# Linear attention and a two-layer block on one core: q ahead of k and a denominator without v in the opening, a bf16 spread, one more batch transposed by DMA, the last tile in two halves

## The chip, the cores and the metric

One core of one Trainium2 chip. The time is device microseconds of one execution, the median of several. The granted clock is the share of its full clock that the profile shows TensorE to have had. The four runs of each kernel in the result lie within 0.15% of each other; in the later jobs those of the kernel before spread over 0.4 to 0.9%, the longest of them (304.88 and 304.77 us) with a mean clock of 0.991. "Faster" and "slower" mean by 2% or more.

## The reference, cut to what matters

```python
phi = lambda x: np.where(x > 0, x, np.exp(x) - 1.0) + 1.0        # q, k, v: (8, 8, 576, 64)
q_p, k_p = phi(q), phi(k)
kv  = einsum('bhsd,bhse->bhde', k_p, v);   z = k_p.sum(axis=2)
attn = einsum('bhsd,bhde->bhse', q_p, kv) / (einsum('bhsd,bhd->bhs', q_p, z)[..., None] + 1e-6)
x = attn.transpose(0, 2, 1, 3).reshape(4608, 512)
h = x @ w_in;  out = (h - np.tanh(h)) @ w_out                     # (512, 2048), (2048, 512)
```

## The kernel before

The dense part runs in nine stages of 512 tokens: a first layer (64 matmuls of 512 columns) and a second (64 more). The attention of batch n+1 is woven into stage n as small pieces, at the end of the tiles of the first layer (`s1`) and of the groups of four matmuls of the second (`s2`). Batch 0 has nothing to hide behind: it is the opening. In the traces each engine's rows come in the order of the program, so where a piece stands in the text decides what it waits behind.

The pieces of a batch have these names: phi of q and of k (ScalarE's exp, then a max and a min on VectorE), q transposed (`qT`), `kv` and z, the denominator and 1/den (`rden`), the numerators (`num`, products of q and kv), the spread (each 1/den copied to all rows of its head), and the scaling of the numerators by it into `xT`, the input of the dense part. `w_in` and `w_out` are the weights of the two layers. TensorE writes its products to PSUM, which the kernel lays out as eight banks (`ps_all`).

```python
    load_k(0); load_q(0); load_v(0)          # all of these are issued from POOL, in this order
    make_identity(nc, ident)
    for g in range(4): load_wi(g)
    nc.gpsimd.memset(sel, 0.0)               # fp32 selector [128, 4, 2, 64], four affine selects
    ...
    load_k(1); load_wo(0); load_q(1); load_wo(1); load_v(1); load_wo(2); load_wo(3)

    def a_spread(b):                         # batches 2 to 7: 1/den through DRAM, broadcast by DMA
        ds = dram.tile([H, 4, J * 16], F32, name="ds")
        for t in range(4): nc.sync.dma_start(out=ds[:, t, :], in_=rden_t[b][32*t:32*t+H, :])
        ...                                  # two broadcasts ds -> rdb
    def a_spread_pe(b, bank0, pairs):        # batches 0 and 1: by TensorE into four PSUM banks
        ...  nc.tensor.matmul(bp[...], sel[r, p], rden_t[b][r], start=True, stop=True)
    ...
        if c == 0:                           # stage 0
            ...
            s2[9].append(num1); s2[11].append(lambda: spread1(0)); s2[13].append(lambda: spread1(1))
            s2[14].append(lambda: a_qphi(2, 0)); s2[15].append(lambda: a_qphi(2, 1))
        if c == 1:
            for n in range(4):               # batch 2 transposed by TensorE in stage 1
                s1[4 + n].append(lambda n=n: a_qT_pe(2, n // 2, attn, (n % 2,)))
        ...
            for p in range(NP + 1): s2[9 + p].append(lambda p=p: a_num(n1, p))   # needs rdb
```

## Time and profile before

| | us |
|---|---|
| median (303.03 to 303.42, 4 runs) | 303.19 |
| first dense matmul | 19.89 |
| stage 0, from there to the first matmul of stage 1 | 33.39 |
| first layer of stage 1 | 19.05 |
| second layer of stage 1 (72.33 to 87.12) | 14.79 |
| stages 2 to 8, to the start of the last output copy (296.45) | 209.33 |
| from that copy to the end of the span | 4.85 |

The lengths add up to the span of 301.3 us. The table is read from starts of instructions: the profile models the ends of matmuls, so a pause of TensorE costs about 0.16 us more, start to start, than the idle time that a row shows (a matmul of 512 columns is drawn 0.38 us long, and the next one starts 0.216 us after it).

### The profile page before, as it was taken

The numbers are of one execution on the slowest core, as the hardware profiler recorded it, in microseconds if no ns is written. First come the engines' busy times: TensorE is split into PE (matmuls) and PEld (weight loads), VectorE is DVE, ScalarE is ACT, GpSimd is POOL, SyncE is SP. The second block draws the span as 40 slices with busy tenths as digits, with TensorE's granted clock in tenths as the row PEclk, the third lists the DMA queues.
The fourth block names the chain that finished last, engine by engine and source line by source line (L and its number), as shares of the span: only waits on it lengthen the run. The fifth ranks groups of instructions, "written<-read, shape, count | busy, mean of one in ns | idle before, by whom it ended". The sixth has DMA issues, their size and how long they took to land.

```text
span 301.3 us, 4706 instructions
## 1 busy us (share of the span) xinstructions
PE 291.9 (97%) x1790; PEld 138.3 (46%) x1790; DVE 180.2 (60%) x304; ACT 149.6 (50%) x230; POOL 52.1 (17%) x91
## 2 busy tenths in 40 slices
PE   8989999989999999999999999999999999999993
PEld 3454454444445444544454445444544444444441
DVE  7658944887557854785478557865681467008500
ACT  3638914954734653565256625662562166136420
POOL 8873263051006000600050003000000000000000
PEclk9999999999999999999999999999999999999999
DMA  6999999677969786967697778477108310130033
GB/s 90 189 207 206 205 207 205 181 120 135 212 111 177 122 200 138 155 116 190 140 151 135 179 148 128 87 173 148 38 4 193 71 35 0 37 86 18 2 70 70
DMA packets 36406, 38.23 MB, mean 127 GB/s; under 512 B 14432, under 2 KB 31008, under 8 KB 35616
## 3 DMA queue, kind: packets, MB, share of 16 engines
q0 software_dynamic: 17600, 18.35, 37.8%
q1 hardware_dynamic: 18784, 19.58, 29.0%
q8 instruction: 14, 0.23, 0.3%
q14 instruction: 8, 0.07, 0.1%
HBM read 43.78 MB, written 9.55 MB: 177 GB/s over the span
## 4 chain that ended last, share of the span: by engine, by line
PE 79%; DMA 9%; DVE 5%; ACT 2%; issue 1%; POOL 1%; SPq 0%; DVEq 0%; POOLq 0%; ACTq 0%
PE ps_all L270 38%; PE ps_all L285 33%; DMA qraw<-in_q_dram 4%; PE ps_all L166 4%; DMA out_dram<-osb 2%; DVE gT L276 2%; PE ps_all L221 2%; DMA v<-in_v_dram 2%; ACT e L127 1%; ACT osb L290 1%; DVE kp L129 1%; PE ps_all L191 1%; POOL kraw L85 1%; DVE r L128 1%; DVE qp L129 1%
## 5 line engine op out<-in xcount | busy, mean ns | idle before, releaser
L285 PE MATMUL ps_all<-w_out_sb,gT 128*128 128x512 bf16 x576 | 131.6, 379 | 0.0
L270 PE MATMUL ps_all<-xT,w_in_sb 128*128 128x512 bf16 x576 | 128.5, 379 | 0.2 <-DVE xT L263 0.2
L276 DVE TENSOR_TENSOR gT<-ps_all,th 128x512 bf16<-128x512 f32 x144 | 96.8, 687 | 53.0 <-ACT th L275 52.6
L275 ACT ACTIVATE th<-ps_all 128x512 f32<-128x512 f32 x144 | 85.3, 600 | 51.7 <-PE ps_all L270 47.2
L285 PEld LDWEIGHTS <-gT 128*128 128x128 bf16 x576 | 55.5, 98 | 65.7 <-issue 0.2
L270 PEld LDWEIGHTS <-w_in_sb 128*128 128x128 bf16 x576 | 55.2, 98 | 65.9 <-issue 1.1
L290 ACT COPY osb<-ps_all 128x512 f32<-128x512 f32 x36 | 21.1, 586 | 79.6 <-PE ps_all L285 59.5
L232 DVE TENSOR_TENSOR xT<-ps_all,rdb 128x512 bf16<-128x512 f32 x24 | 16.4, 689 | 11.8 <-PE ps_all L221 11.8
L104 POOL DMA_DIRECT2D v<-in_v_dram x32 | 19.2, 615 | 18.7 <-PE ps_all L166 5.7
L127 ACT ACTIVATE e<-kraw 128x1152 bf16<-128x1152 bf16 x16 | 18.5, 1165 | 5.1 <-DMA kraw<-in_k_dram 5.1
L129 DVE TENSOR_TENSOR kp<-e,r 128x1152 bf16<-128x1152 bf16 x16 | 12.1, 759 | 14.1 <-ACT e L127 13.0
L127 ACT ACTIVATE e<-qraw 128x1152 bf16<-128x1152 bf16 x16 | 18.4, 1166 | 0.9 <-DMA qraw<-in_q_dram 0.9
L129 DVE TENSOR_TENSOR qp<-e,r 128x1152 bf16<-128x1152 bf16 x16 | 12.1, 758 | 8.1 <-ACT e L127 7.3
L281 POOL COPY g<-gT 1x1 bf16<-1x1 bf16 x4 | 0.7, 176 | 92.9 <-DVE gT L276 92.9
L166 PE MATMUL ps_all<-v,kp 64*128 64x192 bf16 x288 | 13.7, 243 | 0.0
L166 PEld LDWEIGHTS <-kp 64*128 64x128 bf16 x288 | 11.5, 94 | 3.5 <-issue 2.9
L338 PE MATMUL ps_all<-zero 128*128 128x512 bf16 x36 | 10.4, 461 | 1.2 <-DVE zero L297 1.2
L221 PE MATMUL ps_all<-qT,kz 128*128 128x512 bf16 x32 | 11.3, 380 | 0.0
L89 POOL DMA_DIRECT2D kraw<-in_k_dram x14 | 8.7, 628 | 11.8 <-ACT qT L157 10.4
L89 POOL DMA_DIRECT2D qraw<-in_q_dram x14 | 8.7, 642 | 5.9 <-DVE r L128 5.9
L263 DVE TENSOR_TENSOR xT<-ns,ps_all 128x576 bf16<-128x576 f32 x8 | 5.6, 750 | 5.0 <-PE ps_all L258 5.0
L175 DVE TENSOR_TENSOR kz<-ps_all,mask 128x320 bf16<-128x320 f32 x14 | 6.2, 485 | 3.7 <-PE ps_all L166 3.7
(45 smaller groups left out, 92.8 us busy)
## 6 DMA issues: line engine op xcount, KB each, us to landing
out_dram<-osb SPq DMA_DIRECT2D x72, 128.0 KB
rdb<-ds SPq DMA_DIRECT2D x12, 576.0 KB
v<-in_v_dram POOLq DMA_DIRECT2D x32, 144.0 KB, 6.7
kraw<-in_k_dram POOLq DMA_DIRECT2D x14, 288.0 KB, 5.0
qraw<-in_q_dram POOLq DMA_DIRECT2D x14, 288.0 KB, 6.8
w_in_sb<-in_moe_w_in_dram POOLq DMA_DIRECT2D x4, 512.0 KB, 10.1
w_out_sb<-in_moe_w_out_dram POOLq DMA_DIRECT2D x4, 512.0 KB, 12.1
kraw<-in_k_dram POOLq DMA_DIRECT2D x4, 144.0 KB, 3.8
```

The source lines that it names most:

```text
L89: nc.gpsimd.dma_start(out=t[64 * hg:64 * hg + 64].rearrange("p i h j d -> p (i h) (j d)"), in_=src[b, 4 * hg:4 * hg + 4].rearrange("h (p j ...
L104: nc.gpsimd.dma_start(out=v_b[b % 2][64 * hg:64 * hg + 64, i, 0:2].rearrange("p h j d -> p h (j d)"), in_=v[b, h0:h0 + 2].rearrange("h (p ...
L127: nc.scalar.activation(e, x, AF.Exp)
L129: nc.vector.tensor_tensor(store[b][:, i].rearrange("p j h d -> p h j d"), e, r, ALU.min)
L166: nc.tensor.matmul(ps[hg], kp[r, i, j].rearrange("p h d -> p (h d)"), vt[r, i, :, j, :], start=(j == 0), stop=(j == J - 1))
L221: nc.tensor.matmul(ps, kz[:, p // 2, p % 2, 0:128], qT[:, p % 2, 0:8, p // 2, :], start=True, stop=True)
L232: nc.vector.tensor_mul(xT[:, p, S * b:S * b + 512].rearrange("p (j t c) -> p j t c", j=8, t=4), ps.rearrange("p j (t c) -> p j t c", t=4), ...
L270: nc.tensor.matmul(h, w_in_sb[:, p, fi * 128:(fi + 1) * 128], xT[:, p, c * 512:(c + 1) * 512], start=(p == 0), stop=(p == NP - 1))
L275: nc.scalar.activation(th, h, AF.Tanh)
L276: nc.vector.tensor_sub(gT[:, fi, :], h, th)
L285: nc.tensor.matmul(o, gT[:, fi, i * 128:(i + 1) * 128], w_out_sb[:, fi, :], start=(fi == 0), stop=(fi == NF - 1))
L290: nc.scalar.copy(osb, o)
```

## The change

It means to shorten the opening (q first, then k; z from k alone, so that the denominator no longer waits for v; selectors built small), to take TensorE work out (batch 2's transposes; batch 1's spread in bf16 in place of fp32), and to shorten the end. Batch 1's pieces in stage 0 stand a step or two later than before, batch 2's kv and denominator in stage 1 one or two steps earlier. The core of the diff:

```diff
-    load_k(0); load_q(0); load_v(0); make_identity(nc, ident)
+    load_q(0); make_identity(nc, ident); load_k(0); load_v(0)
+    nc.gpsimd.memset(s8, 0.0)                    # three small selectors [128, 3, 4, 2]
+    for n in range(3):
+        for t in range(4): nc.gpsimd.affine_select(out=s8[r, n], ...)
     for g in range(4): load_wi(g)
-    nc.gpsimd.memset(sel, 0.0)
-    for t in range(4): nc.gpsimd.affine_select(out=sel[r], ...)
...                                               # the opening: z, kv, numerators of batch 0 in pieces
+    def a_split(b):                              # 1/den as three bf16 parts, rows 0-7, 8-15, 16-23
...
-  sel[r, p], rden_t[b][r]
+  (sel3 if b else sel)[r, p], rden_t[b][r]       # bf16 for batch 1
...
+            s2[9].append(lambda: (a_den(1, side), a_split(1)))
+            s2[12].append(lambda: spread1(0));  s2[13].append(lambda: a_qphi(2, 0))
+            s2[14].append(lambda: spread1(1));  s2[15].append(lambda: (a_qphi(2, 1), a_qT_dma(2)))
...
-            for n in range(4): s1[4 + n].append(lambda n=n: a_qT_pe(2, n // 2, attn, (n % 2,)))
-            s1[9 if c == 1 else 5].append(lambda: a_kv(n1, attn))
-            s1[11 if c == 1 else 8].append(lambda: (a_den(n1, attn), a_spread(n1)))
+            s1[7 if c == 1 else 5].append(lambda: a_kv(n1, attn))
+            s1[10 if c == 1 else 8].append(lambda: (a_den(n1, attn), a_spread(n1)))
-            s1[3].append(lambda: (a_kphi(2, 1), load_k(3), load_q(3)))   # stage 1
-            if c + 3 < B: s1[10].append(lambda: load_v(c + 3))
+            s1[0].append(lambda: (gate(gT, 0), load_k(n2), load_q(n2), load_v(n2)))
...
+            if c == NC - 1 and i == 3: ...       # last tile in two halves of 256 columns
```

More of the change, by code (lines that the diff above doesn't have):

```diff
@@ L67 @@
     sel = const.tile([128, NP, 2, 64], F32, name="sel")
+    sel3 = const.tile([128, NP, 2, 64], BF16, name="sel3")
+    s8 = const.tile([128, 3, NP, 2], F32, name="s8")
+    part = const.tile([128, 2], F32, name="part")
     zero = const.tile([128, 512], BF16, name="zero")
@@ L118, with phi_pieces @@
     kp_t, qp_t, qT_t, kz_t, rdb_t, rden_t = {}, {}, {}, {}, {}, {}
-    def phi(b, src, store, name, i):
+    def phi_pieces(b, src, store, name, i):
         if i == 0:
@@ L126, in phi @@
         r = epool.tile([128, 2, J, D], BF16, name="r")
-        nc.scalar.activation(e, x, AF.Exp)
-        nc.vector.tensor_scalar(r, x, 0.0, 1.0, ALU.max, ALU.add)
-        nc.vector.tensor_tensor(store[b][:, i].rearrange("p j h d -> p h j d"), e, r, ALU.min)
+        y = store[b][:, i].rearrange("p j h d -> p h j d")
+        return (lambda: nc.scalar.activation(e, x, AF.Exp),
+                lambda: nc.vector.tensor_scalar(r, x, 0.0, 1.0, ALU.max, ALU.add),
+                lambda: nc.vector.tensor_tensor(y, e, r, ALU.min))
+    def phi(b, src, store, name, i):
+        for f in phi_pieces(b, src, store, name, i):
+            f()
     def a_kphi(b, i):
@@ L144, in a_qT_dma, with a_qT_pe @@
             in_=qp_t[b].rearrange("p i j h d -> p (i j h d)"))
-    def a_qT_pe(b, i, banks, parts=(0, 1)):
-        if i == 0 and 0 in parts:
+    def a_qT_pe(b, i, banks, on=None):
+        if i == 0:
             new_qT(b)
-        for n in parts:
+        for n in range(2):
             j0, j1 = ((0, 5), (5, 9))[n]
@@ L155, in a_qT_pe @@
             dst = qT_t[b][:, i, j0:j1].rearrange("p j g t -> p j (g t)")
-            if n == 0:
+            if (on or "AV")[n] == "A":
                 nc.scalar.copy(dst, src)
@@ L175, in a_kv, with b0_z, b0_zc, b0_kv @@
             nc.vector.tensor_mul(kz_t[b][:, hg], ps[hg][:, :, 0:160], mask[:, hg])
-    def a_kv_half(b, i, banks):
-        if i == 0:
-            kz_t[b] = work.tile([128, 2, 2, 160], BF16, name="kz")
-        ps = [banks()[:, 0:192] for hg in range(2)]
-        kv_mm(b, i, ps)
-        for hg in range(2):
-            nc.vector.tensor_mul(kz_t[b][:, hg, i, :], ps[hg][:, 0:160], mask[:, hg, i, :])
+    def b0_z(i):
+        for j in range(J):
+            for hg in range(2):
+                r = slice(64 * hg, 64 * hg + 64)
+                nc.tensor.matmul(ps_all[:, 2 * i + hg, 0:32], kp_t[0][r, i, j].rearrange("p h d -> p (h d)"),
+                                 one[r, 0:32], start=(j == 0), stop=(j == J - 1))
+    def b0_zc(i):
+        nc.vector.tensor_mul(kz_t[0][:, :, i, 128:160], ps_all[:, 2 * i:2 * i + 2, 0:32], mask[:, :, i, 128:160])
+    def b0_kv(i):
+        for j in range(J):
+            for hg in range(2):
+                r = slice(64 * hg, 64 * hg + 64)
+                nc.tensor.matmul(ps_all[:, 4 + 2 * i + hg, 0:128], kp_t[0][r, i, j].rearrange("p h d -> p (h d)"),
+                                 v_b[0][r, i, 0:2, j, :], start=(j == 0), stop=(j == J - 1))
+    def b0_kz(i):
+        nc.vector.tensor_mul(kz_t[0][:, :, i, 0:128], ps_all[:, 4 + 2 * i:6 + 2 * i, 0:128], mask[:, :, i, 0:128])
+    def b0_num(i, ns, rem):
+        kz, qT = kz_t[0], qT_t[0]
+        for hg in range(2):
+            nc.tensor.matmul(ps_all[:, rem, 64 * hg:64 * hg + 64], kz[:, hg, i, 0:128], qT[:, i, 8, hg, :],
+                             start=True, stop=True)
+        for hg in range(2):
+            nc.tensor.matmul(ps_all[:, 4 + hg, :].rearrange("p (j t) -> p j t", j=8), kz[:, hg, i, 0:128],
+                             qT[:, i, 0:8, hg, :], start=True, stop=True)
+        nc.scalar.copy(ns[:, i::2, 8, :], ps_all[:, rem, 0:128].rearrange("p (a t) -> p a t", a=2))
+        nc.scalar.copy(ns[:, i::2, 0:8, :].rearrange("p a j t -> p a (j t)"), ps_all[:, 4:6, :])
     def a_den(b, banks):
@@ L203, in a_den @@
         rden_t[b] = rden
+    def a_split(b):
+        f = rden_t[b]
+        t1 = rpool.tile([128, J * 16], BF16, name="t1")
+        u = rpool.tile([128, J * 16], F32, name="u")
+        t2 = rpool.tile([128, J * 16], BF16, name="t2")
+        w = rpool.tile([128, J * 16], BF16, name="w")
+        nc.vector.tensor_copy(t1, f)
+        nc.vector.scalar_tensor_tensor(u, t1, part[:, 0:1], f, ALU.mult, ALU.add)
+        nc.vector.tensor_copy(t2, u)
+        nc.vector.scalar_tensor_tensor(w, t2, part[:, 1:2], u, ALU.mult, ALU.add)
+        rden_t[b] = w
     def a_spread(b):
@@ L257, in a_spread_pe @@
                 r = slice(32 * t, 32 * t + 32)
-                nc.tensor.matmul(bp[:, t, 144 * n:144 * n + 144], sel[r, p].rearrange("p h e -> p (h e)"),
+                nc.tensor.matmul(bp[:, t, 144 * n:144 * n + 144], (sel3 if b else sel)[r, p].rearrange("p h e -> p (h e)"),
                                  rden_t[b][r], start=True, stop=True)
@@ L266, in a_scale, with l1mm @@
             bp[:, :, o:o + 144].rearrange("p t (j c) -> p t j c", c=16))
-    def l1mm(c, fi, h, p):
+    def l1mm(c, fi, h, p, n):
         nc.tensor.matmul(h, w_in_sb[:, p, fi * 128:(fi + 1) * 128], xT[:, p, c * 512:(c + 1) * 512],
-                         start=(p == 0), stop=(p == NP - 1))
+                         start=(n == 0), stop=(n == NP - 1))
     def l1act(fi, h, gT):
@@ L286, in l2mm, with evac @@
                              start=(fi == 0), stop=(fi == NF - 1))
-    def evac(c, i, o):
+    def evac(c, i, o, f0=0, f1=None):
+        f1 = DM if f1 is None else f1
         osb = opool.tile([128, DM], F32, name="osb")
-        nc.scalar.copy(osb, o)
+        nc.scalar.copy(osb[:, f0:f1], o[:, f0:f1])
         for half in range(2):
             b, j = divmod(2 * (4 * c + i) + half, J)
-            nc.sync.dma_start(out=out[b * S:(b + 1) * S, :].rearrange("(p j) m -> p j m", j=J)[:, j, :],
-                              in_=osb[64 * half:64 * half + 64])
+            nc.sync.dma_start(out=out[b * S:(b + 1) * S, f0:f1].rearrange("(p j) m -> p j m", j=J)[:, j, :],
+                              in_=osb[64 * half:64 * half + 64, f0:f1])
     nc.vector.memset(zero, 0.0)
@@ L299 @@
     nc.scalar.activation(act0, zero[:, 0:1], AF.Exp)
+    load_q(0)
+    make_identity(nc, ident)
     load_k(0)
-    load_q(0)
     load_v(0)
-    make_identity(nc, ident)
+    nc.gpsimd.memset(s8, 0.0)
+    for n in range(3):
+        for t in range(4):
+            r = slice(32 * t, 32 * t + 32)
+            nc.gpsimd.affine_select(
+                out=s8[r, n], in_=s8[r, n], compare_op=ALU.not_equal, fill=1.0, base=-8 * n,
+                channel_multiplier=1, pattern=[[-1, NP], [-4, 2]])
     for g in range(4):
         load_wi(g)
-    nc.gpsimd.memset(sel, 0.0)
-    for t in range(4):
-        r = slice(32 * t, 32 * t + 32)
-        nc.gpsimd.affine_select(
-            out=sel[r], in_=sel[r], compare_op=ALU.not_equal, fill=1.0, base=0,
-            channel_multiplier=1, pattern=[[-1, NP], [-4, 2], [0, 64]])
     load_k(1)
@@ L325 @@
             nc.vector.memset(mask[64 * hh:64 * hh + 64, p // 2, p % 2, m:m + 1], 1.0)
-    for i in range(2):
-        nc.vector.memset(v_b[i][:, :, 2], 1.0)
+    for n in (1, 2):
+        nc.vector.tensor_copy(mask[:, :, :, 128 + 8 * n:136 + 8 * n], mask[:, :, :, 128:136])
     nc.vector.memset(one, 1.0)
@@ L331 @@
     for n in range(3):
-        part = float(np.float32(rest).astype(ml_dtypes.bfloat16))
-        nc.vector.memset(eps[32 * n:32 * n + 1], part)
-        rest -= part
-    for n in range(36):
-        nc.tensor.matmul(ps_all[:, n % 4, :], zero[:, 0:128], zero, start=True, stop=True)
-    for i in range(2):
-        a_kphi(0, i)
-    for i in range(2):
-        a_qphi(0, i)
-    side, kvb = Banks([4, 5, 6, 7]), Banks([0, 1, 2, 3])
-    a_qT_pe(0, 0, side)
-    a_kv_half(0, 0, kvb)
-    a_qT_pe(0, 1, side)
@@ L347 @@
-    ns0 = new_ns(0)
-    for p in (0, 2):
-        a_num_copy(0, ns0, p, side)
-    a_kv_half(0, 1, kvb)
-    a_den(0, Banks([0]))
-    a_num_copy(0, ns0, NP, Banks([1]))
-    for p in (1, 3):
-        a_num_copy(0, ns0, p, side)
-    bp_a = a_spread_pe(0, 0, (0,))
-    bp_b = a_spread_pe(0, 4, (1, 2, 3))
-    for p in range(NP):
-        a_scale(0, p, ns0, bp_b if p else bp_a, 144 * (p - 1) if p else 0)
+        e0 = float(np.float32(rest).astype(ml_dtypes.bfloat16))
+        nc.vector.memset(eps[32 * n:32 * n + 1], e0)
@@ new lines, with spin @@
+        rest -= e0
+    def spin(n):
+        for _ in range(n):
+            nc.tensor.matmul(ps_all[:, 2, :], zero[:, 0:128], zero, start=True, stop=True)
+    side = Banks([4, 5, 6, 7])
+    kz_t[0] = work.tile([128, 2, 2, 160], BF16, name="kz")
+    (eq0, rq0, mq0), (eq1, rq1, mq1) = (phi_pieces(0, q_t, qp_t, "qp", i) for i in range(2))
+    for f in (eq0, rq0, mq0, eq1, rq1):
+        f()
+    spin(18)
+    a_qT_pe(0, 0, side, "AA")
+    (ek0, rk0, mk0), (ek1, rk1, mk1) = (phi_pieces(0, k_t, kp_t, "kp", i) for i in range(2))
@@ new lines @@
+    for f in (mq1, rk0, ek0):
+        f()
+    spin(6)
+    a_qT_pe(0, 1, side, "VV")
+    for f in (ek1, rk1, mk0):
+        f()
+    nc.scalar.copy(sel, s8[:, 0].unsqueeze(3).to_broadcast([128, NP, 2, 64]))
+    spin(8)
+    b0_z(0)
+    mk1()
+    b0_zc(0)
+    b0_kv(0)
+    b0_kz(0)
+    b0_z(1)
+    b0_zc(1)
+    a_den(0, Banks([0]))
+    ns0 = new_ns(0)
+    b0_num(0, ns0, 1)
+    b0_kv(1)
+    bp_a = a_spread_pe(0, 0, (0, 2))
+    b0_kz(1)
+    b0_num(1, ns0, 6)
+    bp_b = a_spread_pe(0, 4, (1, 3))
@@ new lines @@
+    for n, p in enumerate((0, 2, 1, 3)):
+        a_scale(0, p, ns0, (bp_a, bp_b)[n // 2], 144 * (n % 2))
+    nc.vector.memset(v_b[1][:, :, 2], 1.0)
+    nc.vector.memset(v_b[0][:, :, 2], 1.0)
+    s24 = rpool.tile([128, NP, 2], F32, name="s24")
+    nc.vector.tensor_add(s24, s8[:, 1], s8[:, 2])
+    nc.vector.tensor_reduce(part[:, 0:1], s24.rearrange("p a h -> p (a h)"), mybir.AxisListType.X, ALU.add, negate=True)
+    nc.vector.tensor_reduce(part[:, 1:2], s8[:, 2].rearrange("p a h -> p (a h)"), mybir.AxisListType.X, ALU.add, negate=True)
@@ L359 @@
+    nc.vector.tensor_add(s24, s24, s8[:, 0])
+    nc.vector.tensor_copy(sel3, s24.unsqueeze(3).to_broadcast([128, NP, 2, 64]))
     load_q(2)
@@ L375, in spread1 @@
                     a_scale(1, p, sub["ns"], sub["bp"], 144 * (p % 2))
-            s1[11].append(lambda: a_kphi(1, 0))
-            s1[13].append(lambda: a_kphi(1, 1))
-            s1[15].append(lambda: a_qphi(1, 0))
-            s2[1].append(lambda: a_qphi(1, 1))
-            s2[4].append(lambda: a_qT_pe(1, 0, side))
-            s2[5].append(lambda: a_qT_pe(1, 1, side))
-            s2[6].append(lambda: a_kv(1, side))
-            s2[8].append(lambda: a_den(1, side))
             def num1():
@@ L388, in num1 @@
                     a_num_copy(1, sub["ns"], p, side)
-                load_v(3)
-            s2[9].append(num1)
-            s2[11].append(lambda: spread1(0))
-            s2[13].append(lambda: spread1(1))
-            s2[14].append(lambda: a_qphi(2, 0))
-            s2[15].append(lambda: a_qphi(2, 1))
+            s1[13].append(lambda: a_kphi(1, 0))
+            s1[15].append(lambda: a_kphi(1, 1))
+            s2[1].append(lambda: a_qphi(1, 0))
+            s2[3].append(lambda: a_qphi(1, 1))
+            s2[5].append(lambda: a_qT_pe(1, 0, side))
+            s2[6].append(lambda: a_qT_pe(1, 1, side))
+            s2[7].append(lambda: a_kv(1, side))
+            s2[9].append(lambda: (a_den(1, side), a_split(1)))
+            s2[10].append(num1)
+            s2[12].append(lambda: spread1(0))
+            s2[13].append(lambda: a_qphi(2, 0))
+            s2[14].append(lambda: spread1(1))
+            s2[15].append(lambda: (a_qphi(2, 1), a_qT_dma(2)))
         elif n1 < B:
-            s1[9 if c == 1 else 5].append(lambda: a_kv(n1, attn))
-            s1[11 if c == 1 else 8].append(lambda: (a_den(n1, attn), a_spread(n1)))
+            s1[7 if c == 1 else 5].append(lambda: a_kv(n1, attn))
+            s1[10 if c == 1 else 8].append(lambda: (a_den(n1, attn), a_spread(n1)))
             for p in range(NP + 1):
                 s2[9 + p].append(lambda p=p: a_num(n1, p))
-            if c + 3 < B:
-                s1[10].append(lambda: load_v(c + 3))
         if c == 1:
             s1[1].append(lambda: a_kphi(2, 0))
-            s1[3].append(lambda: (a_kphi(2, 1), load_k(3), load_q(3)))
-            for n in range(4):
-                s1[4 + n].append(lambda n=n: a_qT_pe(2, n // 2, attn, (n % 2,)))
+            s1[3].append(lambda: a_kphi(2, 1))
         if c >= 1 and n2 < B:
-            if c > 1:
-                s1[0].append(lambda: (gate(gT, 0), load_k(n2), load_q(n2)))
-            d = 4 if c == 1 else 2
+            s1[0].append(lambda: (gate(gT, 0), load_k(n2), load_q(n2), load_v(n2)))
+            d = 2
             s2[d].append(lambda: a_kphi(n2, 0))
@@ L420 @@
             first = Banks([4, 5, 6, 7, 0, 1, 2, 3])
-            for p in range(NP):
+            for n, p in enumerate((0, 2, 1, 3)):
                 for fi in range(4):
-                    l1mm(c, fi, hs[fi], p)
+                    l1mm(c, fi, hs[fi], p, n)
             for fi in range(4):
@@ L428 @@
             for p in range(NP):
-                l1mm(c, fi, h, p)
+                l1mm(c, fi, h, p, p)
             l1act(fi, h, gT)
@@ L438 @@
                 os_[i] = ps_all[:, i, :] if c == 0 else dense()
+            if c == NC - 1 and i == 3:
+                if g == 0:
+                    o2 = dense()
+                    for u, o in enumerate((os_[i], o2)):
+                        f = slice(256 * u, 256 * u + 256)
+                        for fi in range(NF):
+                            nc.tensor.matmul(o[:, f], gT[:, fi, 384:512], w_out_sb[:, fi, f],
+                                             start=(fi == 0), stop=(fi == NF - 1))
+                        evac(c, i, o, 256 * u, 256 * u + 256)
+                continue
             l2mm(gT, os_[i], i, 4 * g, 4 * g + 4)
```

## The prediction

> **What bounds the kernel now.** I read the page first, then the chain of waits, then a table of stretches cut at the stage borders, then timelines of the two places where TensorE was not fed. The first line of the page and the table say that TensorE is the bound:
>
> ```profile
> PE 291.9 (97%) x1790; PEld 138.3 (46%) x1790; DVE 180.2 (60%) x304; ACT 149.6 (50%) x230; POOL 52.1 (17%) x91
> ...
> 19.89:53.28 33.39, 33.39 (x238) 16.48 (x238) 22.54 (x38) 18.58 (x31) 11.85 (x20) 1.00 1.22 206
> 53.28:72.33 19.05, 17.31 (x136) 8.77 (x134) 15.80 (x29) 13.90 (x22) 4.84 (x8) 1.00 0.82 159
> ...
> 87.28:103.27 15.99, 15.99 (x118) 7.79 (x116) 11.72 (x19) 9.54 (x16) 5.03 (x9) 1.00 0.95 162
> ```
>
> The three stretches are stage 0 (from its first first-layer matmul to the first of stage 1), the first layer of stage 1, and the first layer of stage 2. The second number is the length, the third TensorE's busy time. In stage 0 and stage 2 they are equal: every removed matmul counts there. The first layer of stage 1 takes 3.06 us more than that of stage 2, and 1.74 us of it is idle TensorE. The waits in that stretch name what fed it late, PE transposes of batch 2 whose PSUM banks were still being read:
>
> ```profile
> PE ps_all L153 <- ACT qT L157: 1.0, 1, 1.0
> PE ps_all L153 <- DVE qT L159: 0.7, 1, 0.7
> ```
>
> Before 19.89 us nothing of the dense work runs. The chain of waits through that opening reads:
>
> ```profile
> 14.04 0.68 PE ps_all L153 x9
> 14.71 0.51 PE ps_all L221 x2
> 15.22 0.89 PE ps_all L166 x18
> 16.12 0.32 DVE kz L183
> ...
> 16.49 0.47 PE ps_all L191 x8
> ...
> 17.08 1.07 DVE rden L202
> ...
> 18.28 0.71 PE ps_all L258 x6
> ...
> 19.08 0.77 DVE xT L263
> ```
>
> So: last phi, transposes, kv, mask, denominator, reciprocal, spread, scaling, and then the dense layers, 5.9 us after the last phi (13.98). From 72.33 us on the chain is TensorE alone, to the last output copy at 296.45.
>
> **What the Trainium skill says.** "TensorE: Matmul & The Clock Gate", section "Back-to-back issue gap", gives N/2.4 + 2.5 ns, 215.8 ns for 512 columns; the trace agrees (the chain has 64 in 13.81 us, 215.8 each). For 256 columns that gives 109 ns, so cutting the last tile in two costs about 32*109 - 16*216 = 0.04 us. The same page, section "Architectural detail: the array is 16× 32×32, not 1× 128×128", says that ScalarE and VectorE are strict FIFO; in the timeline each engine's rows follow the program's order, and below it matters twice. "FP8 and Floating Point Precision", section "TensorE Precision Notes", says true fp32 takes four passes; the trace shows the cost, below. "ScalarE: Activation LUTs", section "What ACT_TABLE_LOAD costs", gives 186 + 0.833N ns for an ACTIVATE; the copies of 512 columns measure 586 to 600 against 612, near enough to use it for new sizes: 128 columns 0.29 us, 1024 columns 1.04.
>
> **The change part by part.**
>
> 1. Batch 2's transposes go from TensorE to DMA. That removes 18 matmuls (1.65 us in this stretch) and the waits above (1.74). The first layer of stage 1 then holds what stage 2's holds, so 19.05 falls to about 15.99: **-3.06 us**. The DMA transpose takes 2.75 us on SyncE's queue, and in later batches about as long again to land. It starts after the last phi of q (near 6.5 us after my mark X below) and is needed by the denominator near X+15.8: some 3 to 4 us to spare.
>
> 2. Batch 1's spread in bf16. Now:
>
> ```profile
> 48.31 0.77 PE L258 MATMUL ps_all<-rden,sel 32*128 32x144 f32 x16
> 49.01 0.60 PE L285 MATMUL ps_all<-w_out_sb,gT 128*128 128x512 bf16 x2
> ```
>
> From 48.31 to the next matmul are 0.70 us for 16 recorded fp32 matmuls. In bf16 there are 8; the denominator's 16 bf16 matmuls, also 144 columns and four at a time, take 0.36 us, so 8 take about 0.18. Two calls: 2*(0.70-0.18) = **-1.0 us** on TensorE. Four small VectorE instructions come on between reciprocal and spread, about 1 us in all (144 columns each, the den add is 0.30); the reciprocal used to end 2.1 us before the spread, so that hides.
>
> 3. The order around the end of stage 0. Call X the end of the matmuls of step 12. The steps then are: spread and scaling of two pairs at 12, phi of q2's first half at 13, spread and scaling of the other two at 14, phi of the second half at 15. VectorE is in order: the second two scalings stand behind the min of step 13's phi, which waits for its exp, which stands on ScalarE behind the output copy of step 13. Durations from the trace: copy 0.59, exp 1.17, min 0.76, scaling 0.71. Step 13's matmuls end at X+1.06 (spread 0.2, then 4*0.216), copy to X+1.85, exp to X+3.0, min to X+3.85, scalings to X+4.6 and X+5.3. The first layer of stage 1 would start at X+3.0 and wants pair 2 at X+3.4. So it waits about 1.2 and 0.5 us: **+1.7 us**. Before, both scalings ended (53.10) just as stage 1 began (53.28). This is the wait that takes the place of the one removed.
>
> 4. The opening. Loads arrive in order of issue, the limit being DMA; the first uses of the eight k and q pieces now are at 5.15, 8.5, 10.24 and 11.73 for each half. With q first, q fills the early places and k the late. ScalarE then: exp of q1 to 9.67, two qT copies (0.69+0.59) to 10.95, exp of k0 to 12.1, of k1 to 13.3; VectorE's min of k1 ends near 14.1, about where the last phi ends now. From there, with z as its own narrow matmuls: z1 at 14.4, denominator 15.2 to 15.8, reciprocal to 16.9, first spread to 17.7, first scaling to 18.5. That alone would start the dense layer at about 18.6, 1.3 us earlier. But TensorE's program has more ahead of it: kv1 (to 16.95), num1 after the mask of kv1 (17.6) to 18.2, ScalarE's 128- and 1024-column copies of num1 to about 19.4, and only then the second spread, which writes banks 4 and 5 that this copy reads, with 0.7 us. The dense layer starts at about 20.2: **+0.3 us**, between -1.3 and +0.8.
>
> 5. Removed from the opening: two memsets of 1.02 us and the wide fp32 selector on POOL. They and the bf16 selector, some 3 us of VectorE, now run after the scalings; VectorE is then behind at the start of stage 0 but has 8 banks of room, and at 0.69 against 0.86 us per tile it catches up before the second layer. The twelve small selects on POOL (an estimate: 0.15 us each, between the 0.29 and 0.71 of wider ones) put the weight loads 2 us later in issue; the first was issued at 9.84 and took 7.2 to land, queued behind the inputs, so it should land as before, near 17.1. No effect.
>
> 6. The last tile is cut in two 256-column halves, so the last copy has 256 columns, not 512: 0.37 instead of 0.59 us, and half the bytes in the last two stores. **-0.3 us**.
>
> 7. k, q and v loaded together one stage ahead: VectorE and ScalarE find them early enough as now; no effect.
>
> Sum: -3.06 - 1.0 + 1.7 + 0.3 - 0.3 = -2.4, from 303.2 to 300.8. Point 4 is the only one where I doubt my bookkeeping on both sides, and an order called tuned has probably been measured; I lean 0.5 us to the good there: **300.3 us**.
>
> **The rivals.** (a) The opening really is shortened: the k chain without v's wait gains 1.3 us and the second spread does not hold it up. For it: the change's intent, and 18.6 for the first scaling. Against it: the bank that the second spread shares with num1. Total about 299.2. (b) No wait at the start of stage 1, because the phi at step 13 finds ScalarE free sooner: total about 298.7. Against it: both engines are in order. (c) VectorE becomes the bound of stage 1's first layer: it has 15.8 us of work in the 19.05 now, and the same work would have to fit in 16; with only 6 dense banks a lag of more than 4 us stalls TensorE. Total 301.5. (d) The DMA transpose lands late behind the output stores and holds up the denominator: 1 to 3 us, total 302 to 303.
>
> **Range and chances.** All terms are below 3.1 us. All gains together without any loss, with rival (a), give 303.2 - 3.06 - 1.0 - 1.3 - 0.3 = 297.5; all losses at once give about 303. I take 298.2 to 302.3. More than 2% is 6.1 us, which needs more than everything counted: 5%. Slower by 2% has no mechanism: 2%.
>
> **What would show each step.** The first dense matmul at 20.2 (18.6 if rival a), and what it waited for; two idle gaps of TensorE, 1.2 and 0.5 us, within the first four matmuls of stage 1, released by VectorE's scaling; its first layer at 16 us plus these gaps, no PE transposes in it; 8 bf16 spread matmuls in about 0.2 us; the last copy at 0.37 us. Wrong would make it: a stage-0 transposition of batch 1 that waits for phi of q, now later behind VectorE's new work, or the two DMA rivals.

## The result

302.78 us (302.62 to 303.01, 4 runs) against 303.19 for the kernel before: a ratio of 0.9987, 95% interval 0.9969 to 1.0004, so no change. A ratio here is the mean time of one kernel's fast runs over that of the other's of the same rounds, so not quite the ratio of the medians. The prediction's range was 298.2 to 302.3.

First the engines' line of the page and the table of stretches of the changed kernel, cut at the same events as before: stage 0 and the two layers of stage 1. A row has start and end, the length, then the busy time and count of TensorE, its weight loads, VectorE, ScalarE and POOL, then the granted clock, the DMA share and GB/s.

```profile
PE 288.7 (96%) x1804; PEld 137.2 (46%) x1804; DVE 181.9 (60%) x313; ACT 149.6 (50%) x229; POOL 52.9 (18%) x100
...
20.25:54.08 33.83, 32.63 (x223) 15.63 (x223) 24.00 (x46) 19.53 (x31) 10.47 (x16) 1.00 1.22 207
54.08:71.36 17.28, 16.30 (x117) 7.76 (x116) 16.09 (x28) 12.36 (x20) 5.01 (x9) 1.00 0.93 173
71.36:87.72 16.36, 14.95 (x73) 6.75 (x72) 8.87 (x15) 6.58 (x8) 0.00 (x0) 1.00 0.83 179
```

Before, the first two stretches read as the prediction shows them, and the third:

```profile
72.33:87.12 14.79, 14.79 (x73) 6.78 (x72) 8.76 (x16) 6.58 (x8) 0.00 (x0) 1.00 0.62 137
```

TensorE's busy time fell by 3.2 us, 1.0 of it four warm-up matmuls fewer in the opening. So TensorE has less work. But in each of these three stretches its busy time is now below the length. In stage 0 and the second layer of stage 1 there were no gaps before; in the first layer of stage 1 the old ones (1.74) have given place to others. The list of TensorE's waits names them, as total, count and longest (the warm-up's is left out, and two of 0.5 and 0.4 in the opening):

```profile
PE ps_all L318 <- DMA w_in_sb<-in_moe_w_in_dram: 1.4, 1, 1.4
PE ps_all L269 <- DVE xT L280: 1.4, 1, 1.4
PE ps_all L333 <- DMA w_out_sb<-in_moe_w_out_dram: 1.2, 1, 1.2
...
PE ps_all L306 <- ACT ns L218: 1.1, 1, 1.1
PE ps_all L318 <- DVE xT L311: 1.0, 2, 0.7
```

In order of time: the second spread of the opening waits for a copy (1.1), the first dense matmul for w_in (1.4), the second layer of stage 0 for w_out (1.2), the first matmuls of stage 1 for the scalings (0.7 and 0.3), a numerator of stage 1 for xT (1.4). The account against the kernel before:

| | before | changed | difference | predicted |
|---|---|---|---|---|
| first dense matmul | 19.89 | 20.25 | +0.36 | +0.3 |
| stage 0 | 33.39 | 33.83 | +0.44 | -1.0 |
| first layer of stage 1 | 19.05 | 17.28 | -1.77 | -1.4 |
| second layer of stage 1 | 14.79 | 16.36 | +1.57 | 0 |
| to the last output copy | 209.33 | 209.37 | +0.04 | 0 |
| from it to the end | 4.85 | 4.11 | -0.74 | -0.3 |

The sum is -0.1 us of span, where -2.4 was reckoned. What was not foreseen stands mainly in two places: stage 0, where the bf16 spread's gain was there and a wait for w_out ate it, and the second layer of stage 1, where nothing had been expected.

**The weight loads.** POOL's rows, before:

```profile
9.84 3.00 POOL L110 DMA_DIRECT2D w_in_sb<-in_moe_w_in_dram  x4
12.80 0.78 POOL L306 MEMSET sel<- 128x512 f32 x1
13.65 3.04 POOL L309 TENSOR_SCALAR_AFFINE_SELECT sel<-sel 32x512 f32<-32x512 f32 x4
```

and of the changed kernel:

```profile
9.25 4.22 POOL L358 TENSOR_SCALAR_AFFINE_SELECT s<-s 32x8 f32<-32x8 f32 x12
13.43 3.03 POOL L113 DMA_DIRECT2D w_in_sb<-in_moe_w_in_dram  x4
```

The twelve selects have 8 columns each in place of 512, but they are twelve, take 4.22 us, and now stand ahead of the weight loads, which are issued at 13.43 in place of 9.84. The DMA queues ran dry just then: in quarters of a microsecond the GB/s go from 198 at 12.50 to 14 at 13.50, and are back at 176 only at 16.00, some 2.5 us after the first of these issues began. The stretch from 13 to 16 us, first before, then changed:

```profile
13.00:16.00 3.00, 2.98 (x47) 2.06 (x45) 2.07 (x6) 1.95 (x4) 2.75 (x4) 1.00 1.23 205
```

```profile
13.00:16.00 3.00, 2.83 (x84) 1.82 (x81) 2.31 (x6) 1.28 (x2) 2.95 (x6) 1.00 0.37 35
```

The loads up to stage 0's second layer follow one another at 200 GB/s or so, so what is lost at 13 us is still missing at 38: w_in's first part lands at 20.20 (17.06 before), the second part of w_out at 38.84 (36.23 before).

**The start of stage 1.** VectorE and TensorE in the timeline of the changed kernel (start, length, instruction; in brackets the idle time ahead of it and what ended it):

```profile
53.89 0.76 DVE L133 TENSOR_TENSOR qp<-e,r 128x1152 bf16<-128x1152 bf16 x1 [0.78 <-ACT e L131]
...
54.57 1.41 DVE L311 TENSOR_TENSOR xT<-ns,ps_all 128x576 bf16<-128x576 f32 x2
...
55.37 0.38 PE L318 MATMUL ps_all<-xT,w_in_sb 128*128 128x512 bf16 x1 [0.69 <-DVE xT L311]
...
56.03 6.42 PE L318 MATMUL ps_all<-xT,w_in_sb 128*128 128x512 bf16 x29 [0.29 <-DVE xT L311]
```

The scalings follow the min of the phi, which waited for ScalarE's exp, as step 3 had it. From the first matmul (54.08) to the third (55.37) are 1.29 us instead of 0.43, to the fourth 0.66 instead of 0.22: 1.30 us lost.

**The broadcast of 1/den of batch 2.** In the second layer of stage 1:

```profile
82.98 1.89 DVE L280 TENSOR_TENSOR xT<-ps_all,rdb 128x512 bf16<-128x512 f32 x3 [2.07 <-DMA rdb<-ds]
...
83.72 0.38 PE L269 MATMUL ps_all<-qT,kz 128*128 128x512 bf16 x1 [1.41 <-DVE xT L280]
```

VectorE waits for the DMA `rdb`; the third numerator needs a PSUM bank that VectorE has not read. Before, the first such scaling started at 81.79 with no idle time ahead of it. TensorE now comes to its numerators 0.96 us sooner (80.00 against 80.96), but the broadcast comes later. The four stores of 1/den that it reads go out 1.8 us sooner than before, yet it can be issued only 0.7 us later than before. First before, then changed:

```profile
71.25 1.34 SPq L209 DMA_DIRECT2D ds<-rden  x4
73.68 1.13 SPq L212 DMA_DIRECT2D rdb<-ds  x2
81.79 1.35 DVE L232 TENSOR_TENSOR xT<-ps_all,rdb 128x512 bf16<-128x512 f32 x2
```

```profile
69.43 1.36 SPq L257 DMA_DIRECT2D ds<-rden  x4
74.36 1.13 SPq L260 DMA_DIRECT2D rdb<-ds  x2
```

### The profile page after: what moved, and what is told of

It is laid out like the page before. It is cut to its first block, busy times and chain, and to the rows that moved or that the text cites. A ratio compares the mean times of both kernels' runs of the same rounds, so it can differ in the third digit from the quotient of the medians.

```text
span 301.2 us, 4766 instructions
## 1 busy us (share of the span) xinstructions
PE 288.7 (96%) x1804; PEld 137.2 (46%) x1804; DVE 181.9 (60%) x313; ACT 149.6 (50%) x229; POOL 52.9 (18%) x100
## 4 chain that ended last, share of the span: by engine, by line
PE 79%; DMA 14%; DVE 2%; POOL 2%; ACT 1%; issue 1%; SPq 0%; DVEq 0%; ACTq 0%; POOLq 0%
PE ps_all L318 35%; PE ps_all L333 35%; DMA w_out_sb<-in_moe_w_out_dram 5%; PE ps_all L174 4%; DMA w_in_sb<-in_moe_w_in_dram 3%; DMA rdb<-ds 3%; PE ps_all L269 2%; DMA kraw<-in_k_dram 2%; DMA ds<-rden 1%; PE ps_all L515 1%; POOL qraw L88 1%; ACT e L131 1%; PE ps_all L226 1%; POOL kraw L88 1%; DVE xT L311 0%
## 5 line engine op out<-in xcount | busy, mean ns | idle before, releaser
L333 PE MATMUL ps_all<-w_out_sb,gT 128*128 128x512 bf16 x560 | 128.3, 379 | 1.2 <-DMA w_out_sb<-in_moe_w_out_dram 1.2
L333 PEld LDWEIGHTS <-gT 128*128 128x128 bf16 x560 | 54.0, 98 | 66.7 <-issue 3.3
L339 ACT COPY osb<-ps_all 128x512 f32<-128x512 f32 (+1 forms) x37 | 21.2, 574 | 78.4 <-PE ps_all L333 58.7
L131 ACT ACTIVATE e<-kraw 128x1152 bf16<-128x1152 bf16 x16 | 18.6, 1163 | 0.5 <-DMA kraw<-in_k_dram 0.5
L174 PE MATMUL ps_all<-v,kp 64*128 64x192 bf16 x252 | 11.6, 243 | 0.0
L269 PE MATMUL ps_all<-qT,kz 128*128 128x512 bf16 x28 | 10.1, 379 | 1.4 <-DVE xT L280 1.4
L174 PEld LDWEIGHTS <-kp 64*128 64x128 bf16 x252 | 10.0, 94 | 3.0 <-issue 2.5
L390 PE MATMUL ps_all<-zero 128*128 128x512 bf16 x32 | 9.4, 455 | 1.2 <-DVE zero L346 1.2
L132 DVE TENSOR_SCALAR r<-qraw 128x1152 bf16<-128x1152 bf16 x16 | 7.4, 464 | 2.3 <-DMA qraw<-in_q_dram 2.3
```

What stands on the lines that cost most here:

```text
L131: return (lambda: nc.scalar.activation(e, x, AF.Exp), lambda: nc.vector.tensor_scalar(r, x, 0.0, 1.0, ALU.max, ALU.add), lambda: nc.vector ...
L174: nc.tensor.matmul(ps[hg], kp[r, i, j].rearrange("p h d -> p (h d)"), vt[r, i, :, j, :], start=(j == 0), stop=(j == J - 1))
L269: nc.tensor.matmul(ps, kz[:, p // 2, p % 2, 0:128], qT[:, p % 2, 0:8, p // 2, :], start=True, stop=True)
L333: nc.tensor.matmul(o, gT[:, fi, i * 128:(i + 1) * 128], w_out_sb[:, fi, :], start=(fi == 0), stop=(fi == NF - 1))
L339: nc.scalar.copy(osb[:, f0:f1], o[:, f0:f1])
```

## The experiments

All gave correct results. The jobs ran on different chips, so each time is given with its ratio to the kernel before in the same rounds.

**1. Weight loads ahead of the selects** (`wi_first`).

```diff
     load_v(0)
+    for g in range(4): load_wi(g)
     nc.gpsimd.memset(s8, 0.0)
     ...                                   # twelve affine_selects
-    for g in range(4): load_wi(g)
```

> The changed kernel with the four loads of w_in issued before the twelve small selects on POOL, nothing else. Theory W (the selects delay the weight loads, the loads are in series behind them, and two of TensorE's waits come from that): the first dense matmul starts near 18.8 us in place of 20.25, held then by the second spread, and the wait of 1.20 us for w_out in the second layer of stage 0 is gone; 2.6 us less than the changed kernel, near 300.2. Rival G (given back): the wait of 1.41 us in the second layer of stage 1, for the broadcast of 1/den, grows by as much as is gained before it, since its transfers queue behind the loads; the time stays near 302.5.

300.54 us, ratio 0.9929 (0.9915 to 0.9943): by the ratios 1.8 us less than the changed kernel, where 2.6 was expected. Neither wait for a weight is in the trace any more; the wait on xT in stage 1 is 1.4 as before, so nothing was given back there. The first dense matmul starts at 19.48, not 18.8: k's last half was used 0.7 us later in this run than in the changed kernel (11.91 against 11.21), why I did not find out; over the kept fast traces of this opening that use falls anywhere from 11.21 to 12.03. Theory W holds.

**2. The second scalings ahead of the phi** (`scale_first`).

```diff
-            s2[13].append(lambda: a_qphi(2, 0))
-            s2[14].append(lambda: spread1(1))
+            s2[14].append(lambda: (spread1(1), a_qphi(2, 0)))
```

> The changed kernel with the phi of the first half of q of batch 2 put behind the second two scalings of batch 1, in step 14, nothing else. Theory S (VectorE's order makes the wait at the start of stage 1): the two gaps of 0.69 and 0.29 us in the first four matmuls of stage 1 shrink to 0.2 or less in all, and the time falls by 0.8 us to near 302.0. Rival G: the gaps go, but the wait for the broadcast of 1/den in stage 1 grows from 1.41 to near 2.2 us, and the time stays near 302.8.

304.1 us, ratio 1.0034 (1.0011 to 1.0057): 0.3% above the kernel before, which neither theory had. The gaps at the start of stage 1 are gone. The wait on xT has grown, as the rival said, and the table of stretches shows what follows it (the granted clock is 0.50):

```profile
PE ps_all L269 <- DVE xT L280: 2.1, 1, 2.1
...
84.10:87.50 3.40, 3.30 (x13) 1.37 (x12) 1.25 (x2) 0.00 (x0) 0.00 (x0) 0.50 0.71 163
```

After the wait of 2.1 us TensorE ran at half its clock for 3.4 us. In the five slower runs the granted mean was 0.989 to 0.997; the one at 0.998 took 302.22. That the wait brings the half clock on is argued from this order of events, not shown: see runs 3 and 12.

**3. The numerators of batch 2 two steps later** (`num_late`).

```diff
-                s2[9 + p].append(lambda p=p: a_num(n1, p))
+                s2[(11 if c == 1 else 9) + p].append(lambda p=p: a_num(n1, p))
```

> The changed kernel with the five numerator steps of batch 2 two steps later in the second layer of stage 1, nothing else. Theory N (the numerator comes before the broadcast of 1/den has landed): the wait of 1.41 us of TensorE on VectorE's xT there goes, and the time falls by 1.4 us to near 301.4. Rival: the last numerators then come so late that the first layer of stage 2 waits for xT by as much; no gain.

301.44 us, ratio 0.9969 (0.9947 to 0.9991), with one run of 303.35 at a clock of 0.994. That is 0.5 us less than the changed kernel by the ratios, 1.6 by the spans of the two traces, where 1.4 was expected. The wait on xT is gone, and stage 2 does not wait in its place. In this trace the dense part began earlier (19.32, no wait for w_in) and the wait for w_out was 2.0 us instead of 1.2: w_out's arrival held that point at 38.84 whatever came before.

**4. The three edits together** (`all_three`).

> The three edits together: w_in loads first, second scalings before the phi, numerators of batch 2 two steps later. If the four waits of the changed kernel (1.41, 1.20, 0.98, 1.41 us) are what hid its gain, they go together: about 4.8 us less than the changed kernel, near 298.0, and TensorE has no wait over 0.3 us after its first dense matmul. Rival G: less than 3 us is kept, because a new wait comes in at the transfers.

298.48 us, ratio 0.9861 (0.9846 to 0.9876), 1.4% under the kernel before: outside the noise, though under 2%. Against the changed kernel it is 3.8 us by the ratios and 4.5 by the spans of the traces (301.2 and 296.7), where 4.8 was expected and rival G had less than 3. In its list of TensorE's waits nothing over 0.2 us is left after the first dense matmul:

```profile
PE ps_all L191 <- DVE kp L133: 1.4, 1, 1.4
...
PE ps_all L306 <- ACT ns L218: 1.1, 1, 1.1
```

Both stand in the opening. The second is the one of the prediction's step 4: the second spread waits for the copy of num1 and starts at 18.88, so the dense part starts at 19.59 here.

**5. The kernel before with batch 2's DMA transpose alone** (`only_dma_t`).

```diff
-            s2[15].append(lambda: a_qphi(2, 1))
+            s2[15].append(lambda: (a_qphi(2, 1), a_qT_dma(2)))
-            for n in range(4): s1[4 + n].append(lambda n=n: a_qT_pe(2, n // 2, attn, (n % 2,)))
```

> The kernel before with one part of the change alone: batch 2's transposes by DMA, issued after its q phi at the end of stage 0, and the PE transposes taken out of stage 1. The prediction's step 1 says 3.06 us less than before, near 300.1, no other wait. Rival D (the broadcast of 1/den of batch 2 lands no earlier, since its small stores queue behind the loads of batch 3): TensorE gets to the numerators of stage 1 up to 3 us earlier and waits there for xT by 1 to 2 us; only 1 to 2 us are kept, near 301.5.

304.22 us, ratio 1.0037 (1.001 to 1.0064). The part with the largest gain on paper brings none when it stands alone. The first layer of stage 1 is 16.38 us long instead of 19.05. Then:

```profile
PE ps_all L221 <- DVE xT L232: 2.2, 1, 2.2
...
82.76:86.18 3.42, 3.42 (x10) 1.22 (x9) 2.74 (x5) 0.00 (x0) 0.00 (x0) 0.50 0.18 34
```

The second layer takes 18.88 us instead of 14.79. Rival D holds, and a half clock after the wait makes it worse: five of six runs had a mean clock of 0.992 to 0.994 and took 304.1 to 304.5, the sixth, at 0.997, took 302.07.

The traces also show why the broadcast lands no earlier, though no load was moved in the text. Before, POOL held the next v back until batch 2's kv product had read the old one. Without the transposes that product comes some 3 us sooner, and v goes out right behind k and q, as it does in the changed kernel (64.37). First before, then this run:

```profile
66.29 2.39 POOL L104 DMA_DIRECT2D v<-in_v_dram  x4 [2.71 <-PE ps_all L166]
```

```profile
63.21 2.42 POOL L104 DMA_DIRECT2D v<-in_v_dram  x4
```

The stores of 1/den then landed 4.1 us after the last one's issue (3.7 in the changed kernel); before, the broadcast itself was issued 1.1 us after it.

**6. The same with the numerators two steps later** (`dma_t_late`).

> The kernel before with the DMA transposes of batch 2 alone, and its numerators two steps later in stage 1. If the 3.06 us of the prediction's step 1 are there and only the wait for the broadcast (2.24 us, and half the clock for 3.4 us after it) ate them, the time falls to near 300.3, with at most 0.4 us of wait left and no drop of the clock. Rival: the removed matmuls were not on the path to the end; the time stays at 302.5.

300.74 us, ratio 0.9916 (0.9889 to 0.9942), 2.2 us under the kernel before by the medians; a wait of 0.2 us on xT, no drop of the clock. So most of step 1's gain is real; it was lost at the broadcast.

**7. The bf16 spread undone in the changed kernel** (`fp32_spread`): the fp32 selector and reciprocal for batch 1, four selects, no `a_split`, no `sel3`.

> The changed kernel with the bf16 spread of batch 1 undone: fp32 selector and reciprocal as for batch 0, four selects on POOL in place of twelve, no split instructions. If the bf16 spread costs more by its eight selects (some 2 us in which no weight load is issued) than it saves on TensorE, this is faster than the changed kernel: the two spreads cost 0.94 us more, the waits for w_in and w_out (1.41 and 1.20 us) are nearly gone; 1.5 us less, near 301.2. Rival: the wait for the broadcast in stage 1 grows by as much, or the bf16 spread is worth its 0.94 us; then 302.8 or more.

301.67 us (300.89 to 305.64), ratio 0.9994 with an interval of 0.9951 to 1.0037: unclear as a time, because one run fell to a clock of 0.994 and took 305.64; the other five took 300.89 to 302.82. The trace has no wait for a weight, and the first dense matmul at 19.21.

**8. The bf16 spread undone in the three edits** (`all_fp32`), where the selects stand behind the loads.

> The three edits together with the bf16 spread of batch 1 undone; here the selects no longer stand ahead of the weight loads. If step 2 of the prediction has its size right, TensorE has 0.94 us more in stage 0 and the time is 0.9 to 1.0 us over the three edits, near 299.4 (ratio 0.989). Rival: the split instructions and selector copies cost what the bf16 matmuls save; ratio 0.986 as with it.

299.56 us, ratio 0.988 (0.9855 to 0.9906), against 298.48 and 0.9861. The medians differ by 1.1 us, but the intervals overlap and the jobs differ. In the traces one spread call takes 0.70 us from start to the next matmul in fp32 and 0.24 in bf16, twice. Stage 0 is 33.41 us long in this trace (19.01 to 52.42) and 32.51 in run 4's (19.59 to 52.10); the traces of runs 7 and 1 have 33.41 and 32.47. So the bf16 spread is worth its 0.9 us on TensorE as soon as its selectors are not in the way.

**9. v of batch 3 after the stores of 1/den** (`v_late`).

```diff
-            s1[0].append(lambda: (gate(gT, 0), load_k(n2), load_q(n2), load_v(n2)))
+            s1[0].append(lambda: (gate(gT, 0), load_k(n2), load_q(n2)))
+            s1[11 if c == 1 else 0].append(lambda: (gate(gT, 11 if c == 1 else 0), load_v(n2)))
```

> The changed kernel with v of batch 3 loaded later in stage 1, after the stores of 1/den of batch 2 (gated by tile 11, not tile 0), nothing else. Theory L (those small stores wait in the DMA queues behind the loads of k, q and v issued together): they land some 2 us earlier, the broadcast also, and the wait of 1.41 us on xT in the second layer of stage 1 falls below 0.5; near 301.6. Rival: the broadcast shares the engines with the v loads that now run beside it and lands as late as before; no change from 302.8.

303.18 us, ratio 1.0001 (0.9978 to 1.0025). The two chains of waits, first of the changed kernel, then of this run; each row is start, length, transfer:

```profile
70.49 3.71 DMA ds<-rden
...
74.89 7.96 DMA rdb<-ds
```

```profile
70.57 1.34 DMA ds<-rden
...
72.60 10.51 DMA rdb<-ds
```

The stores did land 2.3 us earlier, as theory L had it; the broadcast, now beside the v loads, took 2.5 us longer and ended at 83.11 instead of 82.86. The wait was 1.6. As to the time, theory L fell: order alone gains nothing here.

**10. v of batch 3 after the broadcast** (`v_after`): as in 9, but v is loaded at step 11 of the second layer, gated by the first scaled numerator.

> The changed kernel with v of batch 3 loaded only after the first numerator of batch 2, so that neither the stores nor the broadcast of 1/den of batch 2 share the DMA engines with it. Theory Q (the broadcast is late by the amount of loads ahead of it and beside it, not by its own chain): it lands 2 us earlier or more, the wait of 1.41 us on xT in the second layer of stage 1 is gone, near 301.4. Rival: the broadcast takes its 8 us alone (two transfers of 576 KB with output stores beside them) and the wait stays over 1 us.

301.8 us, fast runs 301.33 to 301.95, ratio 0.9952 (0.9927 to 0.9978). Its one trace (clock 0.849) can't be compared.

**11. The same in place of the later numerators, with the two other edits** (`v_after_two`).

> The weight loads first and the second scalings before the phi, as in the three edits together, but with v of batch 3 loaded after the first numerator of batch 2 in place of the later numerators. Theory Q (volume of loads ahead and beside): from the first store of 1/den to the landing of the broadcast 11 us or less, against 13.4 in the changed kernel, the wait on xT below 0.5 us where it would be over 2 with v in the old place, and the time near 298.5. Rival: the broadcast takes as long without v; a wait of 2 us or more on xT, perhaps half the clock after it, 300.5 or more.

298.0 us (one run of 300.71 at a clock of 0.993), ratio 0.985 (0.9817 to 0.9883), as good as the three edits. With the numerators at their old steps there is no wait on xT. The first store goes out at 66.08, and VectorE uses the broadcast at 77.49 without having waited for it: at most 11.4 us, against 13.4 in the changed kernel (69.43 to 82.86). So the volume of loads ahead of and beside the broadcast is what made it late; theory Q holds, though by an upper bound. Two edits besides it were in this run, and the same two with v in its old place were not run; the kernel before, where v went out later, points the same way (71.25 to 81.79 without a wait, at most 10.5 us).

**12. The cut of the last tile undone**, in the changed kernel (`no_tail`) and in the three edits (`all_no_tail`): `if False:` in place of `if c == NC - 1 and i == 3:`.

> The changed kernel with the cut of the last tile undone. The prediction's step 6 gave the cut 0.3 us; the trace of the changed kernel shows 4.1 us from the start of the last output copy to the end of the span against 4.85 before, so undoing should cost 0.6 us: near 303.4.

> The three edits together with the cut of the last tile undone. From the last output copy to the end of the span 4.86 us (uncut) against 4.12 (cut), less 0.05 us for the narrower matmuls: 0.7 us more than with the cut, a ratio to the kernel before near 0.988 against 0.9861; the prediction's 0.3 us would make 0.987.

303.77 us, ratio 1.0044 (1.001 to 1.0078), with clocks of 0.987 to 0.999, and 299.46 us, ratio 0.9868 (0.9839 to 0.9898), with one run of 615 us, the traced one, left out as slow. The times don't settle so small a term. The fast traces do, from the start of the last output copy to the end of the span (301.3, 301.2 and 301.8 us): 4.85 before, 4.11 changed, 4.8 with the cut undone. These are the copies before and in the changed kernel:

```profile
296.45 0.59 ACT L290 COPY osb<-ps_all 128x512 f32<-128x512 f32 x1 [2.87 <-DMA out_dram<-osb]
```

```profile
297.09 0.37 ACT L339 COPY osb<-ps_all 128x256 f32<-128x256 f32 x1 [1.37 <-PE ps_all L515]
```

The trace of `no_tail` also bears on the clock. It ran at half clock from about 20.3 to 23.7 us, though the pauses of TensorE just before were only 1.1 (the second spread) and 0.6 us (w_in):

```profile
21.00:23.00 2.00, 2.00 (x6) 0.76 (x5) 1.77 (x5) 0.00 (x0) 0.74 (x1) 0.50 1.24 205
```

So the length of one wait does not decide it: 1.1 and 0.6 us were followed by it here, 2.0 us in run 3 was not.

## Why the prediction was wrong, point by point

- **Step 1, the transposes to DMA: size nearly right, but "-3.06" was booked as if it reached the end.** The first layer of stage 1 is 17.28 us, less 1.30 of step 3's wait 15.98, against 15.99 named. Where that wait is really gone (runs 2, 4 and 11) the layer is 16.29, and in run 5 16.38, so 2.7 to 2.8 of the 3.06 us are seen. (The two parts it names, 1.65 and 1.74, add to 3.39; the 3.06 came from comparing two stages.) What failed is that nobody asked what TensorE would meet next when it came sooner. It met the broadcast of 1/den of batch 2, whose time is set by DMA traffic and not by TensorE: 1.57 us lost in the changed kernel, 2.2 us of wait and half a clock in the run of this part alone. That is the first of two steps that failed.
- **Step 2, bf16 spread: right.** 0.24 against 0.70 us per call, 0.9 of the 1.0 named.
- **Step 3, the wait at the start of stage 1: mechanism right, size 1.30 for 1.7.** Exp and min came a little sooner than in the sum. Run 2 shows that the order makes it: with the order changed the layer is 0.99 us shorter (16.29). What it is worth in time once the broadcast is out of the way was run only together with the other edits (runs 4 and 11).
- **Step 4, the opening: the number 20.2 is right (20.25) by luck, the reason is not.** The inputs came sooner than I had read from the uses before: the first scaling began at 16.49, not 17.7. (The copies of 128 and 1024 columns took 0.27 and 1.01 us, against 0.29 and 1.04.) The second spread did wait for the copy of num1 (1.1 us), but had passed by 18.77. What held the dense part from there to 20.25 was w_in. In runs 3 and 9, whose opening is the same text, it began at 19.32 and 19.40 without that wait, and the wait for w_out was longer instead (2.0 and 1.9).
- **Step 5, "No effect" of the selects on the weight loads: the second step that failed.** They were put at 2 us and took 4.22 (0.20 each and 0.05 between as a rule, four longer); the estimate of 0.15 each lies below both of the selects that it is said to lie between. And "queued behind the inputs" did not hold: w_in was issued 3.59 us later and landed 3.14 us later (20.20 against 17.06), since the queues ran dry as it was issued. Two waits came of it, 1.48 us (18.77 to 20.25) and, far from the cause, 1.35 us in the second layer of stage 0 (8 matmuls from 35.80 would end at 37.53; the next began at 38.88). Run 1 takes both away with one edit.
- **Step 6, the tail: -0.74 for -0.3.** The copy is 0.22 us shorter, as named; the last stores end about 0.5 us sooner, which I had not put a number on.
- **Step 7, loading k, q and v together: no wait on them, right as far as it went,** but their share of DMA engines is what the broadcast competes with, which the step left out. Runs 10 and 11 show it, and run 5 shows that v can move up behind q without any edit to the loads.
- **The rivals.** (a) fell: with w_in out of the way (run 1) the second spread still waited 1.1 us, and the dense part began at 19.48, not 18.6; (b) fell, the wait was there; (c) did not come; (d) came for the broadcast and not for the transpose, with the size it named. (The totals are not on one base: (a)'s 299.2 starts from 300.8, (b)'s 298.7 from the lowered 300.3.)

The sum from the runs: the four waits of the changed kernel cost 1.48 + 1.35 + 1.30 + 1.57 = 5.7 us, which is why a kernel with some 3 us of matmuls and PE waits less, and a shorter tail, took the same time. Run 4 got back 4.5 us of span and not 5.7, since its dense part began 0.66 us sooner and not 1.48 (the second spread held it), and 0.99 of the 1.30 came back.

## What to carry to other kernels

When a stage is made shorter, list what the next stage waits for that does not come from the shortened engine, above all transfers, and ask when each lands; the gain ends at the first of them, and the earlier stage can itself move other transfers up in front of it. In a queue of loads in series, a few microseconds of other work in the issuing engine's program become a hole that every later load inherits, so put address and selector set-up behind the issues. Where TensorE is left waiting for a microsecond or two, look at the clock after it: in run 5 the second layer of stage 1 lost 4.1 us, 2.4 to the wait and 1.7 to the half clock.

## What the Trainium skill lacked or had wrong

- "TensorE: Matmul & The Clock Gate", section "What's actually happening", has the clock fall to half after at least one idle window of about 3.4 us. Here waits of 2.1 and 2.2 us were followed by 3.4 us at a granted clock of 0.50 (84.10 to 87.50, 82.76 to 86.18), while 2.0 us in run 3 and 1.4 us in the changed kernel were not, and in `no_tail` pauses of 1.1 and 0.6 us were followed by about as long at 0.50 (20.3 to 23.7). So the half clock came without a pause as long as the window that it states; what else brings it on these runs do not show.
- "SBUF — State Buffer", section "Who interferes with whom", says that POOL and VectorE share a port pair as an exclusive lock. The selects agree: 0.20 us each as a rule, but 0.62 and 0.79 for the two that ran beside VectorE's mins of k at 11.57 to 13.16. No page has what a small select costs; here it is 0.20 us plus 0.05 between, so twelve of 8 columns (4.22 us) cost more than four of 512 (3.04).
- "DMA: Bandwidth & Descriptors", section "Queues, rings and completion order", says that each DMA engine takes turns between queues, packet by packet. Small stores issued while a queue of loads was full landed 3.7 us after the last one's issue, and 1.3 us when v was not ahead of them; I can't tell from the traces which part of the path they waited in.
